# Softmax probabilities of 24 heads kept in one PSUM bank, and a maximum over partitions taken by TensorE

## The chip, the cores and the metric

The kernel runs on one core of a Trainium2 chip. The metric is the time of one execution on the device in microseconds (us); the number quoted is the median of three runs. A separate profiled execution gives the trace from which all rows here are read. The engines are named as in the profile: PE (TensorE, matmuls), DVE (VectorE), ACT (ScalarE), POOL (GpSimd) and SP (SyncE, which here only issues DMAs). "Span" is the time from the first to the last instruction in the trace.

## What is computed

A causal attention with a decay, whose output is the input of a small mixture of experts:

```python
B, H, S, D = 4, 8, 576, 64
scores = q @ k^T / sqrt(D)
scores = where(causal, -1e9, scores + cum[:, :, :, None] - cum[:, :, None, :])   # cum = cumsum(log f)
attn   = exp(scores - max(scores));  attn = attn / (sum(attn) + 1e-9)
x      = (attn @ v)  reshaped to [2304, 512]
p      = domain_probs / (domain_probs.sum(-1) + 1e-9)
out    = sum over e in 0..3 of  p[:, e] * (max(x @ w1[e], 0) @ w2[e])            # w1 512x1024, w2 1024x512
```

The float32 data is multiplied as pairs of a high and a low half (`hi`/`lo`, mostly float16), so that one product is three matmuls. For float16 each tensor is scaled by a power of two, found at run time from the largest magnitude in it.

## The kernel before

**Jobs and heads.** Attention works by job: a batch `b` (0 to 3), a pair of heads `pr` (0 to 3) and a half. A first half is the queries 0 to 255 (tiles 0 and 1 of 128 rows), a second half the queries 256 to 575 (tiles 2, 3, 4). First halves of all four batches run first, then the second halves. A job has two heads, so there are 64 entries in `heads`. Entries 0 to 7 (batch 0) run alone in a start-up; entries 8 to 31 are the first halves of batches 1 to 3, and these 24 heads are what the change speaks of first. They run woven with steps of the expert matmuls: `Step.l1` (L1077, first layer), `Step.gate` (ACT L1090 writes `gh`, DVE L1091 writes `gl`), `Step.l2` (L1113, second layer) and the addition of a finished result to `acc` (DVE, L1137 or L1142).

**One head.** A head of the 24 takes these steps, for tile 0 (128 keys) and tile 1 (256 keys):

- `qk_pe`: two matmuls (L638) put the scores in a PSUM tile `s`. Before the change each query tile has its own `s`, so a head takes two PSUM banks.
- `qk_min`: one custom instruction on DVE (L652) reads `s` and the mask, writes the scaled scores to an SBUF tile `p`, and keeps the row minimum in `nm` (a second small row with the name `nm` reads the accumulator).
- `qk_exp`: ACT (L667) computes the exponential of `p` in place, with `nm` as bias, and sums a row into `ss`.
- `recip16`: DVE turns the two sums of the head into factors `rs` (L702, L705).
- `turn16`: ACT (L748) writes the high half of `p * rs` to the float16 buffer `z`, DVE (L749) the low half; then SP issues two transposing DMAs (L761) that put `z` into `pt`.
- later `av_pair` (PE, L848) multiplies `pt` by v, and `out16` (ACT, DVE L902) splits the result into `y`.

**PSUM.** There are eight banks of 512 float32 columns. `ps_a` has four buffers, which `s`, the attention outputs `o` and a few small tiles (`top...`) take in turn; `ps_1` and `ps_2` have two each, for the two expert layers. The SBUF pool `p_p` for `p` has six buffers.

**Scale of v.** For batches 0 to 3 an upper bound on the attention output is made from v (`x_bound`), batch by batch. Since the second halves use one common scale, `v_scale` (L390) combines them: `top` takes the maximum over the columns of `vmax` (DVE, L398 and L401), which leaves 128 numbers on 128 partitions. To reduce over partitions, SP writes them to DRAM (`dv`, L402) and reads them back as one row copied to every partition (`tops`, L403). `finish` then takes the maximum of that row on DVE, cuts it to a power of two, and makes `vsc` and `xun` (L408 to L421). `weigh` (POOL, L442) for later chunks and the split of v for second halves need the result. `top` belongs to the list `bounds[30]`, `finish` to `bounds[31]`, that is, to the last two of the 24 heads.

The helper `power` (L200) does the same reduction for the bounds of the batches and for the weights: PE transposes the column into a PSUM tile (L206), DVE reduces that row and cuts it to a power of two (L209 to L220), PE multiplies by ones to copy it to all partitions (L227), and DVE reads it (L236, L239).

**Order.** Heads and expert steps are put in a sequence by a planner that paces attention steps between matmuls; from it, a scheduler orders the instructions of each engine when the program is built. Each engine then runs its list strictly in that order, and waits at an instruction until what it needs is there. SP's list is one queue of DMA issues.

Of the kernel before, what the change touches and what calls it, by code (L numbers as in the profile page):

```python
# [85 lines left out]
def fused(ctx: ExitStack, tc: tile.TileContext, qk, v, f, probs, w, out):  # L86
# [42 lines left out]
    xun = const.tile([128, 8], F32, name="xun")  # L129
    tops = const.tile([128, 256], F32, name="tops")  # L130
    pr_r = tops[:, : NT // 128 * E].rearrange("p (t e) -> p t e", e=E)
    ones_r = const.tile([4, 128], F32, name="ones_r")
# [257 lines left out]
    def v_scale():  # L390

        m = vmax[:, NV : NV + 1]
        d = dr_p.tile([128, 1], F32, tag="dv", name="dv", bufs=1)
        u = vmax[:, NV + 1 : NV + 2]

        def top():
            assert all(("x", b) in known for b in range(B))
            nc.vector.tensor_tensor(  # L398
                out=vmax[:, :B], in0=vmax[:, :B], in1=xsc[:, :B], op=ALU.max
            )  # L400
            nc.vector.tensor_reduce(out=m, in_=vmax[:, :NV], op=ALU.max, axis=AX.X)  # L401
            nc.sync.dma_start(out=d, in_=m)  # L402
            nc.sync.dma_start(  # L403
                out=tops[:, :128], in_=d.rearrange("q k -> (q k)").partition_broadcast(128)
            )

        def finish():
            nc.vector.tensor_reduce(out=u, in_=tops[:, :128], op=ALU.max, axis=AX.X)  # L408
            nc.vector.tensor_scalar(out=u, in0=u, scalar1=TINY, scalar2=None, op0=ALU.max)
            nc.vector.tensor_scalar(  # L410
                out=u.bitcast(I32),
                in0=u.bitcast(I32),
                scalar1=EXPONENT,
                scalar2=None,
                op0=ALU.bitwise_and,
            )
            nc.vector.reciprocal(out=vsc[:, B : B + 1], in_=u)
            nc.vector.tensor_scalar(
                out=xun[:, B : B + 1], in0=u, scalar1=2.0**-2, scalar2=None, op0=ALU.mult
            )  # L420
            nc.vector.tensor_scalar(  # L421
                out=vsc[:, B : B + 1],
                in0=vsc[:, B : B + 1],
                scalar1=2.0**14,
                scalar2=None,
                op0=ALU.mult,
            )
            known.add(("x", B))

        return top, finish  # L430

# [81 lines left out]
    class Job:  # L513


        def __init__(self, b, pr, half):
# [4 lines left out]
            self.njt = 2 if half == 0 else 5  # L521
            self.pairs = b > 0 or half > 0
            self.nm = f"{b}_{pr}_{half}"
            self.hi, self.kl, self.q2, self.p, self.nmax = {}, {}, {}, {}, {}
# [86 lines left out]
        def begin(self, hh):  # L611
            for t in self.its:
                self.p[hh, t] = p_p.tile([128, S], F32, tag="p", name=f"p{self.nm}_{hh}_{t}")
            self.nmax[hh] = st_p.tile([128, 8], F32, tag="nmax", name=f"nm{self.nm}_{hh}")
            if hh == 0:
                n = len(self.its)
                self.ssum = st_p.tile([128, 2, n], F32, tag="ssum", name=f"ss{self.nm}")
                self.rs = st_p.tile([128, 2, n], F32, tag="rs", name=f"rs{self.nm}")

        def qk_pe(self, hh, its):  # L620

            at = 512
            for t in its:
# [3 lines left out]
                for n, (a, z) in enumerate(cuts):  # L627
# [4 lines left out]
                    for m, (lhsT, rhs) in enumerate(  # L632
# [11 lines left out]
                        )  # L644
                    self.sp.setdefault((hh, t), []).append((a, z, ps[:, at : at + z - a]))
                    at += z - a

# [28 lines left out]
        def qk_tile(self, hh, t):  # L676
            self.qk_pe(hh, (t,))
            self.qk_min(hh, t)
# [252 lines left out]
    parts_v = v_scale()  # L931
    bounds[30] = [(50, parts_v[0])]
    bounds[31] = [(50, parts_v[1])]

# [901 lines left out]
```

## Time and profile before

| | us |
|---|---|
| median of three runs | 935.0 |
| range of the three | 934.6 to 940.25 |
| the profiled execution | 933.63 |
| its span in the trace | 931.8 |

The 24 heads run from about 53 to about 245 us of the span; in that stretch stands nearly all of PE's idle time after the start-up. In the rows further below, `L652` is a line of the kernel before; `out<-in` names the tiles without their buffer numbers; `x24` is a count; `[10.38 <-DMA tops<-dv]` is idle time of the engine just before the instruction, and what ended it. A wait for several things is put down to the one that came last.

### The profile page before, as it was taken

Reading aid. Unit: us, or ns where it says so; the run is one execution under the profiler, and the core shown is the slowest. Engines: PE = TensorE matmul, PEld = TensorE weight load, DVE = VectorE, ACT = ScalarE, POOL = GpSimd, SP = SyncE. Lnnn points to the kernel's source line nnn. Section 1 sums busy time; section 2 is a strip of 40 time slices with the busy share of each in tenths; the row PEclk is TensorE's granted clock in tenths of the full one; section 3 lists DMA queues with packets and bytes.
Section 4 is the critical chain, followed back from the end, with each engine's and each line's share of the span. In section 5 each row is a group of like instructions: output and inputs, shape, how many; then the busy total and the mean of one; then the engine's idle time right before and its main releaser. Section 6 shows DMA issues by size and latency. Waiting matters only on the chain.

```text
span 931.8 us, 16630 instructions
## 1 busy us (share of the span) xinstructions
PE 866.4 (93%) x5756; PEld 570.8 (61%) x5756; DVE 712.5 (76%) x1496; ACT 544.4 (58%) x1118; POOL 463.9 (50%) x496
## 2 busy tenths in 40 slices
PE   3698989879999998999999899999998999999998
PEld 2577756446667665676766576654455664666547
DVE  5589799836888899878888867655678747786487
ACT  5766849435676685665767765445655345653350
POOL 3746645344325275325238520384778627885060
PEclk9999999989999999999999999999999999999999
DMA  8667889949999999985897984254322422241003
GB/s 281 197 180 235 232 273 250 256 120 270 252 236 258 228 255 276 238 235 125 209 286 228 299 184 76 56 187 140 114 74 91 159 91 89 70 124 36 24 1 91
DMA packets 167236, 163.64 MB, mean 176 GB/s; under 512 B 105108, under 2 KB 129872, under 8 KB 167152
## 3 DMA queue, kind: packets, MB, share of 16 engines
q1 hardware_dynamic: 167152, 162.58, 62.8%
q8 instruction: 45, 0.74, 0.3%
q14 instruction: 39, 0.32, 0.1%
HBM read 116.78 MB, written 21.64 MB: 149 GB/s over the span
## 4 chain that ended last, share of the span: by engine, by line
PE 48%; POOL 9%; DVE 8%; ACT 6%; issue 3%; DMA 1%; SPq 0%; POOLq 0%; ACTq 0%; DVEq 0%
PE l L1077 13%; PE l L1113 13%; PE y L1348 8%; PE m L1348 8%; PE s L638 4%; POOL s L1408 4%; POOL wt L1245 3%; PE o L848 3%; POOL wu L1245 1%; DVE z L749 1%; DVE rl L1234 1%; ACT wt L1272 1%; DVE acc L1142 1%; DVE h L1383 1%; ACT r L1394 1%
## 5 line engine op out<-in xcount | busy, mean ns | idle before, releaser
L1077 PE MATMUL l<-y,w 128*128 128x256 f16 x1728 | 213.9, 274 | 2.1 <-DVE w L1044 2.1
L1077 PEld LDWEIGHTS <-w 128*128 128x128 f16 x1728 | 162.7, 98 | 43.6 <-issue 7.4
L1113 PE MATMUL l<-w,gh 128*128 128x512 f16 x568 | 173.6, 389 | 9.6 <-DVE acc L1142 9.6
L667 ACT ACTIVATE p<-p,nm 128x576 f32<-128x576 f32 (+2 forms) x160 | 95.7, 599 | 87.2 <-DVE nm L652 74.9
L586 POOL CAST q<-raw 64x320 fp32r<-64x320 f32 (+1 forms) x56 | 27.0, 482 | 193.3 <-issue 88.5
L749 DVE SCALAR_TENSOR_TENSOR z<-p,rs,z 128x384 f16<-128x384 f32 (+5 forms) x176 | 109.5, 645 | 16.6 <-ACT z L748 15.3
L1113 PE MATMUL l<-w,gl 128*128 128x512 f16 x284 | 108.4, 387 | 6.9 <-DVE gl L1091 6.9
L748 ACT ACTIVATE z<-p,rs 128x384 f16<-128x384 f32 (+5 forms) x176 | 88.6, 550 | 31.5 <-issue 17.7
L1142 DVE SCALAR_TENSOR_TENSOR acc<-y,scg,acc 128x256 f32<-128x256 f32 (+1 forms) x164 | 81.2, 516 | 14.9 <-PE y L1348 14.7
L1113 PEld LDWEIGHTS <-gh 128*128 128x128 f16 x568 | 51.5, 99 | 60.2 <-issue 19.3
L638 PE MATMUL s<-hi 128*128 128x384 f32 (+1 forms) x192 | 77.1, 409 | 10.9 <-POOL hi L600 5.8
L652 DVE CUSTOM_DVE_ANT_0 p<-s,mask 128x288 f32<-128x288 f32 (+2 forms) x160 | 74.2, 474 | 16.4 <-PE s L638 16.1
L1348 PE MATMUL m<-rh,bs 128*128 128x512 f16 x256 | 86.4, 379 | 0.2 <-POOL bs L1277 0.2
L594 POOL TENSOR_TENSOR kl<-raw,hi 64x576 fp32r<-64x576 f32 (+1 forms) x56 | 66.2, 1182 | 17.8 <-ACT hi L585 17.1
L1277 POOL TENSOR_TENSOR bs<-wt,bs 128x512 f16<-128x512 f32 x32 | 37.9, 1190 | 73.4 <-ACT bs L1276 73.0
L1091 DVE SCALAR_TENSOR_TENSOR gl<-l,gh 128x512 f16<-128x512 f32 (+1 forms) x80 | 54.7, 684 | 16.3 <-ACT gh L1090 15.6
L1348 PE MATMUL m<-rh,bw 128*128 128x512 f16 x191 | 64.5, 379 | 1.0 <-ACT r L1394 0.9
L585 ACT ACTIVATE hi<-raw 128x896 fp32r<-128x896 f32 (+1 forms) x56 | 45.3, 808 | 34.3 <-DMA raw<-in_qk 13.7
L638 PE MATMUL s<-kl,q 66*128 66x384 f32 (+1 forms) x192 | 61.6, 327 | 0.0
L1348 PEld LDWEIGHTS <-bs 128*128 128x128 f16 x384 | 37.5, 98 | 38.8 <-POOL bs L1277 0.7
L1383 DVE SCALAR_TENSOR_TENSOR h<-s,h 128x512 f16<-128x512 f32 x40 | 46.4, 1165 | 17.8 <-ACT h L1382 17.5
L1348 PEld LDWEIGHTS <-h 128*128 128x128 f16 x480 | 46.9, 98 | 14.8 <-issue 2.6
(389 smaller groups left out, 1889.2 us busy)
## 6 DMA issues: line engine op xcount, KB each, us to landing
wr<-in_w SPq DMA_DIRECT2D x74, 512.0 KB
wd<-w SPq DMA_DIRECT2D x32, 512.0 KB
w<-wd SPq DMA_DIRECT2D x32, 512.0 KB
raw<-in_qk SPq DMA_DIRECT2D x32, 448.0 KB
wp<-in_w SPq DMA_DIRECT2D x32, 256.0 KB
bv<-wd SPq DMA_DIRECT2D x32, 256.0 KB
bw<-wd SPq DMA_DIRECT2D x32, 256.0 KB
raw<-in_qk SPq DMA_DIRECT2D x24, 256.0 KB
```

What stands on the lines that cost most here:

```text
L594: eng.tensor_tensor(out=kl[:64, :wk], in0=r[:64, ko : ko + wk], in1=hi[:64, ko : ko + wk].bitcast(F32), op=ALU.subtract,)
L638: nc.tensor.matmul(out=ps[:, at : at + z - a], lhsT=lhsT, rhs=rhs, start=(m == 0), stop=(m == 1),)
L652: nc.vector.tensor_tensor_reduce(out=pt[:, a:z], in0=ps, in1=mask[:, m0 + a : m0 + z], scale=-0.125, scalar=BIG if n == 0 else nm[:, col : ...
L667: nc.scalar.activation(out=pt[:, :w_], in_=pt[:, :w_], func=AF.Exp, scale=-1.0, bias=self.nmax[hh][:, c : c + 1], accum_out=self.ssum[:, h ...
L748: nc.scalar.activation(out=o[:, 0], in_=x, func=AF.Copy, scale=sc)
L749: nc.vector.scalar_tensor_tensor(out=o[:, 1], in0=x, scalar=sc, in1=o[:, 0], op0=ALU.mult, op1=ALU.subtract)
L1077: nc.tensor.matmul(out=self.l1p[:, fi, :], lhsT=lhsT, rhs=rhs[:, k, :], start=(k == 0 and m == 0), stop=(k == 3 and m == 2),)
L1091: self.last = nc.vector.scalar_tensor_tensor(out=self.gl, in0=self.l1p, scalar=0.0, in1=self.gh.bitcast(F32) if wide else self.gh, op0=ALU ...
L1113: matmul(out=l2[tt], lhsT=lhsT, rhs=rhs, start=(opens and fi == 0 and m == 0), stop=(closes and fi == 1 and m == 2),)
L1142: nc.vector.scalar_tensor_tensor(out=acc[c][:, tt, d0:d1], in0=ps, scalar=sc, in1=acc[c][:, tt, d0:d1], op0=ALU.mult, op1=ALU.add,)
L1348: line.append(nc.tensor.matmul(**args))
L1383: nc.vector.scalar_tensor_tensor(out=t[:, 1], in0=x, scalar=0.0 if relu else 1.0, in1=t[:, 0], op0=op, op1=ALU.subtract,)
```

## The change

**First part.** For jobs with `b > 0` and `half == 0` (`stays`), the `p` tiles are not taken. `qk_pe` is called once for both query tiles, so that their scores (128 + 256 = 384 columns) lie side by side in one PSUM bank, and `p` is that piece of PSUM: `qk_min` and `qk_exp` work in place in PSUM, and `turn16` reads PSUM.

**Second part.** `v_scale` uses `power` for the reduction over partitions, so the two DMAs and the buffer `tops` go. It has three parts now, in `bounds[29]` to `bounds[31]`.

```diff
@@ def v_scale():
         m = vmax[:, NV : NV + 1]
-        d = dr_p.tile([128, 1], F32, tag="dv", name="dv", bufs=1)
-        u = vmax[:, NV + 1 : NV + 2]
+        def use(u, r):
+            nc.vector.tensor_scalar(
+                out=xun[:, B : B + 1], in0=u, scalar1=2.0**-2, scalar2=None, op0=ALU.mult
+            )
+            nc.vector.tensor_scalar(
+                out=vsc[:, B : B + 1], in0=r, scalar1=2.0**14, scalar2=None, op0=ALU.mult
+            )
+            known.add(("x", B))
...
             nc.vector.tensor_reduce(out=m, in_=vmax[:, :NV], op=ALU.max, axis=AX.X)
-            nc.sync.dma_start(out=d, in_=m)
-            nc.sync.dma_start(
-                out=tops[:, :128], in_=d.rearrange("q k -> (q k)").partition_broadcast(128)
-            )
-        def finish():
-            nc.vector.tensor_reduce(out=u, in_=tops[:, :128], op=ALU.max, axis=AX.X)
-            nc.vector.tensor_scalar(out=u, in0=u, scalar1=TINY, scalar2=None, op0=ALU.max)
...
-            known.add(("x", B))
-        return top, finish
+        across, exponent, finish = power(1, m, "v", use)
+        return lambda: (top(), across()), exponent, finish
@@ class Job, __init__
+            self.stays = b > 0 and half == 0
@@ def begin
-                self.p[hh, t] = p_p.tile([128, S], F32, tag="p", name=f"p{self.nm}_{hh}_{t}")
+                if not self.stays:
+                    self.p[hh, t] = p_p.tile([128, S], F32, tag="p", name=f"p{self.nm}_{hh}_{t}")
@@ def qk_pe
+                    if self.stays:
+                        self.p[hh, t] = ps[:, at : at + z - a]
@@ def qk_tile
-            self.qk_pe(hh, (t,))
+            if not self.stays:
+                self.qk_pe(hh, (t,))
+            elif t == self.its[0]:
+                self.qk_pe(hh, self.its)
@@
-    bounds[30] = [(50, parts_v[0])]
-    bounds[31] = [(50, parts_v[1])]
+    for n in range(3):
+        bounds[29 + n] = [(50, parts_v[n])]
```

A third edit only renames: `pr_r`, a view of `tops` before, has a tile `pr_t` of its own.

**What moves.** On PE only the instructions from about the 120th to the 2070th stand in another order, which is the stretch of the 24 heads; behind that the lists agree. PE gets two instructions more (a transpose and a matmul for `topv`), SP loses one row (the two DMAs of v; the issue of one other DMA falls into another row), DVE loses one.

DVE, first pair of heads of batch 1 (`s1_0_0_0...` is head 0, `s1_0_0_1...` head 1; the digit after the head is the query tile before the change, while after it both tiles are in one `s`; `ux` is a step of a bound). Before:

```order
L652 ISA p1_0_0_0_0_587,nm1_0_0_0_589<-s1_0_0_0_0_0_657,mask_112 128x128
L652 ISA p1_0_0_0_1_588,nm1_0_0_0_589<-s1_0_0_0_1_0_683,mask_112 128x256
L652 ISA p1_0_0_1_0_702,nm1_0_0_1_704<-s1_0_0_1_0_0_714,mask_112 128x128
L702 TENSOR_SCALAR ss1_0_0_590<-ss1_0_0_590 128x2
L705 RECIPROCAL rs1_0_0_591<-ss1_0_0_590 128x2
L652 ISA p1_0_0_1_1_703,nm1_0_0_1_704<-s1_0_0_1_1_0_731,mask_112 128x256
L749 SCALAR_TENSOR_TENSOR z0_691<-p1_0_0_0_0_587,rs1_0_0_591,z0_691 128x128
L749 SCALAR_TENSOR_TENSOR z0_691<-p1_0_0_0_1_588,rs1_0_0_591,z0_691 128x2x128
```

After:

```order
L637 ISA s1_0_0_0_0_0_656,nm1_0_0_0_588<-s1_0_0_0_0_0_656,mask_112 128x128
L637 ISA s1_0_0_1_0_0_710,nm1_0_0_1_700<-s1_0_0_1_0_0_710,mask_112 128x128
L637 ISA s1_0_0_0_0_0_656,nm1_0_0_0_588<-s1_0_0_0_0_0_656,mask_112 128x256
L637 ISA s1_0_0_1_0_0_710,nm1_0_0_1_700<-s1_0_0_1_0_0_710,mask_112 128x256
L690 TENSOR_SCALAR ss1_0_0_589<-ss1_0_0_589 128x2
L693 RECIPROCAL rs1_0_0_590<-ss1_0_0_589 128x2
L737 SCALAR_TENSOR_TENSOR z0_689<-s1_0_0_0_0_0_656,rs1_0_0_590,z0_689 128x128
L737 SCALAR_TENSOR_TENSOR z1_690<-s1_0_0_1_0_0_710,rs1_0_0_590,z1_690 128x128
L737 SCALAR_TENSOR_TENSOR z0_689<-s1_0_0_0_0_0_656,rs1_0_0_590,z0_689 128x2x128
```

(L637 of after is L652 of before, L690 is L702, L693 is L705, L737 is L749; the rows that only read an accumulator and those of other work are left out.) The minima of the two heads alternate now, tile by tile, and so do the low halves.

ACT at the same place before:

```order
L667 ACTIVATE p1_0_0_0_0_587,ss1_0_0_590<-p1_0_0_0_0_587,nm1_0_0_0_589 128x128
L667 ACTIVATE p1_0_0_0_1_588,ss1_0_0_590<-p1_0_0_0_1_588,nm1_0_0_0_589 128x256
L585 ACTIVATE hi1_1_0_1_759<-raw1_1_0_1_712 128x512
L667 ACTIVATE p1_0_0_1_0_702,ss1_0_0_590<-p1_0_0_1_0_702,nm1_0_0_1_704 128x128
L748 ACTIVATE z0_691<-p1_0_0_0_0_587,rs1_0_0_591 128x128
L748 ACTIVATE z0_691<-p1_0_0_0_1_588,rs1_0_0_591 128x2x128
```

ACT there after:

```order
L652 ACTIVATE s1_0_0_0_0_0_656,ss1_0_0_589<-s1_0_0_0_0_0_656,nm1_0_0_0_588 128x128
L567 ACTIVATE hi1_1_0_1_752<-raw1_1_0_1_708 128x512
L652 ACTIVATE s1_0_0_1_0_0_710,ss1_0_0_589<-s1_0_0_1_0_0_710,nm1_0_0_1_700 128x128
L652 ACTIVATE s1_0_0_0_0_0_656,ss1_0_0_589<-s1_0_0_0_0_0_656,nm1_0_0_0_588 128x256
L652 ACTIVATE s1_0_0_1_0_0_710,ss1_0_0_589<-s1_0_0_1_0_0_710,nm1_0_0_1_700 128x256
L736 ACTIVATE z0_689<-s1_0_0_0_0_0_656,rs1_0_0_590 128x128
```

In the built program DVE and ACT take turns on a bank: the exponential of tile 0 waits for its minimum, the minimum of tile 1 waits for the exponential of tile 0, and so on through the four high and low halves. Over the 24 heads DVE has 23 waits for ACT more than before (164 instead of 141) and ACT 23 for DVE more (104 instead of 81). On PE, the scores of a later head wait for the last low half of an earlier head, since its bank comes free only then; before, they waited for an earlier head's minimum.

DVE at the scale of v before (`acc0` is the evacuation of an expert result, L1142; its `scg` comes from `weigh`):

```order
L749 SCALAR_TENSOR_TENSOR z0_691<-p3_0_0_0_0_2236,rs3_0_0_2240,z0_691 128x128
L408 TENSOR_REDUCE vmax_122<-tops_126 128x1
L409 TENSOR_SCALAR vmax_122<-vmax_122 128x1
L410 TENSOR_SCALAR vmax_122<-vmax_122 128x1
L749 SCALAR_TENSOR_TENSOR z0_691<-p3_0_0_0_1_2237,rs3_0_0_2240,z0_691 128x2x128
L417 RECIPROCAL vsc_123<-vmax_122 128x1
L418 TENSOR_SCALAR xun_125<-vmax_122 128x1
L421 TENSOR_SCALAR vsc_123<-vsc_123 128x1
L1142 SCALAR_TENSOR_TENSOR acc0_1097<-l2_6_6_0_0_0_2381,scg_128,acc0_1097 128x512
L1142 SCALAR_TENSOR_TENSOR acc0_1097<-l2_6_6_0_0_1_2388,scg_128,acc0_1097 128x512
```

DVE at the scale of v after, some 30 instructions later in its list:

```order
L209 TENSOR_REDUCE uv_173<-topv_172 1x1
L555 SCALAR_TENSOR_TENSOR v23_2_0_2569<-vh3_1511,vsc_123,v23_2_0_2569 128x4x64
L637 ISA s3_2_0_1_0_0_2658,nm3_2_0_1_2638<-s3_2_0_1_0_0_2658,mask_112 128x128
L637 ISA nm3_2_0_1_2638 128x1
L210 TENSOR_SCALAR uv_173<-uv_173 1x1
L637 ISA s3_2_0_0_0_0_2597,nm3_2_0_0_2566<-s3_2_0_0_0_0_2597,mask_112 128x256
L637 ISA nm3_2_0_0_2566 128x1
L213 TENSOR_SCALAR uv_173<-uv_173 1x1
L220 TENSOR_SCALAR uv_173<-ident_111,uv_173 1x1
```

The evacuations `acc0` of step 6 no longer stand behind the reduction. `vmax` itself (L401 before) is ready some 65 rows ahead of its transpose on PE, and the result is read (L236) 20 DVE rows behind this reduction.

## Rows read from the trace of the kernel before

**Rows 1.** The page's first part: busy time of each engine over the span.

```profile
PE 866.4 (93%) x5756; PEld 570.8 (61%) x5756; DVE 712.5 (76%) x1496; ACT 544.4 (58%) x1118; POOL 463.9 (50%) x496
```

**Rows 2.** Waits of PE, 53 to 245 us: line, waited for, total us, times, longest.

```profile
PE l L1113 <- DVE acc L1142: 9.4, 3, 6.1
PE l L1113 <- DVE gl L1091: 5.0, 6, 1.5
...
PE topx L227 <- DVE ux L220: 1.8, 2, 1.6
```

**Rows 3.** Windows: length, busy by engine (count), TensorE's granted clock, DMA share, GB/s.

```profile
275.00:300.00 25.00, 25.00 (x184) 17.07 (x181) 21.64 (x55) 16.43 (x34) 16.09 (x17) 1.00 0.90 237
...
168.20:171.70 3.50, 2.95 (x7) 1.04 (x8) 3.50 (x7) 0.79 (x2) 1.13 (x2) 0.51 1.25 239
...
194.30:200.40 6.10, 0.03 (x1) 0.00 (x0) 1.98 (x9) 0.00 (x0) 0.69 (x3) 0.88 0.25 22
200.40:205.80 5.40, 4.62 (x11) 1.41 (x11) 4.70 (x12) 1.47 (x5) 5.40 (x9) 0.50 0.81 188
...
362.40:366.80 4.40, 4.38 (x17) 2.37 (x18) 2.27 (x6) 3.85 (x9) 1.40 (x2) 0.61 0.86 250
```

**Rows 4.** Timeline of PE at three places: start, length, operation, idle before it.

```profile
166.82 0.59 PE L1113 MATMUL l<-w,gh 128*128 128x512 f16 x2 [2.20 <-DVE acc L1142]
...
200.40 1.87 PE L1113 MATMUL l<-w,gh 128*128 128x512 f16 x4 [6.07 <-DVE acc L1142]
...
362.42 0.40 PE L638 MATMUL s<-hi 128*128 128x288 f32 x1 [4.13 <-DVE nm L652]
```

**Rows 5.** Timeline of SP's issues, 186 to 200 us.

```profile
186.88 0.34 SPq L402 DMA_DIRECT2D dv<-vmax  x1
193.81 0.32 SPq L403 DMA_DIRECT2D tops<-dv  x1
194.22 6.40 SPq L761 DMA_TRANSPOSE pt<-z  x2
```

**Rows 6.** Timeline of DVE at two places, about 164 and 187 to 201 us.

```profile
163.90 2.20 DVE L749 SCALAR_TENSOR_TENSOR z<-p,rs,z 128x128 f16<-128x128 f32 x1
...
187.62 0.35 DVE L749 SCALAR_TENSOR_TENSOR z<-p,rs,z 128x128 f16<-128x128 f32 x1
198.35 0.29 DVE L408 TENSOR_REDUCE vmax<-tops 128x1 f32<-128x128 f32 x1 [10.38 <-DMA tops<-dv]
...
199.60 1.41 DVE L1142 SCALAR_TENSOR_TENSOR acc<-l,scg,acc 128x512 f32<-128x512 f32 x2
```

**Rows 7.** Timeline of POOL, at 163.7 us.

```profile
163.70 2.26 POOL L1039 TENSOR_TENSOR w<-wr,w 128x512 f16<-128x512 f32 x2
```

**Rows 8.** DVE's groups, 53 to 245 us: busy us, mean ns, idle before.

```profile
L749 DVE SCALAR_TENSOR_TENSOR z<-p,rs,z 128x128 f16<-128x128 f32 x24 | 12.8, 535 | 1.2 <-ACT z L748 1.2
L749 DVE SCALAR_TENSOR_TENSOR z<-p,rs,z 128x256 f16<-128x256 f32 x24 | 12.7, 531 | 0.1
```

**Rows 9.** DVE's groups, whole span: operations that read PSUM, and two forms of the minimum.

```profile
L1142 DVE SCALAR_TENSOR_TENSOR acc<-y,scg,acc 128x256 f32<-128x256 f32 x140 | 63.5, 477 | 14.9 <-PE y L1348 14.7
L1142 DVE SCALAR_TENSOR_TENSOR acc<-l,scg,acc 128x512 f32<-128x512 f32 x64 | 47.0, 742 | 1.4 <-PE l L1113 0.9
...
L652 DVE CUSTOM_DVE_ANT_0 p<-s,mask,nm 128x288 f32<-128x288 f32 x32 | 16.4, 513 | 2.8
...
L652 DVE CUSTOM_DVE_ANT_0 p<-s,mask 128x288 f32<-128x288 f32 x32 | 14.4, 450 | 8.0 <-PE s L638 7.9
```

**Rows 10.** Waits of DVE, 53 to 245 us: line, waited for, total us, times, longest.

```profile
DVE ss L702 <- ACT p L667: 9.4, 7, 2.5
...
DVE z L749 <- ACT z L748: 1.2, 3, 0.5
```

**Rows 11.** ACT's groups, 53 to 245 us: the exponential of tile 0.

```profile
L667 ACT ACTIVATE p<-p,nm 128x128 f32<-128x128 f32 x24 | 9.4, 392 | 21.0 <-DVE nm L652 16.5 <-DVE uw L239 2.5 <-DVE ux L210 2.0
```

More of the change, by code (lines that the diff above doesn't have):

```diff
@@ L129, in fused @@
     xun = const.tile([128, 8], F32, name="xun")
-    tops = const.tile([128, 256], F32, name="tops")
-    pr_r = tops[:, : NT // 128 * E].rearrange("p (t e) -> p t e", e=E)
+    pr_t = const.tile([128, NT // 128 * E], F32, name="pr_t")
+    pr_r = pr_t.rearrange("p (t e) -> p t e", e=E)
     ones_r = const.tile([4, 128], F32, name="ones_r")
@@ L401, in top @@
             nc.vector.tensor_reduce(out=m, in_=vmax[:, :NV], op=ALU.max, axis=AX.X)
-            nc.sync.dma_start(out=d, in_=m)
-            nc.sync.dma_start(
-                out=tops[:, :128], in_=d.rearrange("q k -> (q k)").partition_broadcast(128)
-            )
-        def finish():
-            nc.vector.tensor_reduce(out=u, in_=tops[:, :128], op=ALU.max, axis=AX.X)
-            nc.vector.tensor_scalar(out=u, in0=u, scalar1=TINY, scalar2=None, op0=ALU.max)
[L410 to L427, printed above, removed]
-            known.add(("x", B))
-        return top, finish
+        across, exponent, finish = power(1, m, "v", use)
+        return lambda: (top(), across()), exponent, finish
     weighed = set()
```

## The prediction

> **What bounds the kernel now.** First the page's busy times: PE works 866.4 us of the span, 93%, and no other engine comes near [rows 1]. So time can be won only where PE stands idle or runs at its lower clock. A table of windows then shows where that is not: at 275 to 300 us PE is busy 25.00 of 25 us [rows 3], and so it is over most of the later stretches. The stretch of the 24 heads is the exception. PE's waits there, 53 to 245 us, are nine groups; seven of them wait for DVE and sum to 19.6 us. Three of them are shown [rows 2]: 9.4 us in 3 waits for the evacuation `acc`, 5.0 us in 6 for `gl`, 1.8 us in 2 for the scale of a batch; the other four sum to 3.4. The timeline of PE shows that one event makes most of the first: 6.07 us ahead of 200.40 us [rows 4]. DVE is the engine waited for, so I then read what DVE waits for and where it is merely slow.
>
> **What stops PE at 200 us.** DVE ends a low half at 187.62 us and then waits 10.38 us for `tops` [rows 6]. The issues on SP say why [rows 5]: `dv` to DRAM goes out at 186.88, the reading back can be issued only at 193.81, and the reduction starts at 198.35. That is 11.5 us for one maximum over partitions. Behind the reduction on DVE stand the two `acc` evacuations of 199.60 us [rows 6]; PE needs their banks and stops. SP's queue is stopped too: the transposes behind the DMA pair go out at 194.22 us. After its pause PE runs at a granted clock of 0.50, the lower of its two levels: in the 5.40 us from 200.40 it is busy 4.62 us [rows 3].
>
> **Term 1: the scale of v.** The change takes out both DMAs and DVE's wait; in the new order the `acc` evacuations stand ahead of the reduction. PE wins its pause, 6.07 us. It also wins what the half clock cost: 4.62 us of work at clock 0.50 would take 2.3 us at full clock, so 2.3 us. Together **−8.4**. What comes in is one transpose and one matmul on PE and three small DVE operations in place of others. The same chain runs seven times before the change (three bounds, four weight scales) and holds PE for 1.8 us in two waits of the batches' bounds [rows 2]; here the transpose stands 65 rows behind the `vmax` that it needs, and the result is read 20 DVE rows after the reduction, so I take 0, with 1 us as the other bound. Who consumes the result, `weigh` for chunk 4 and the v of second halves, stands far behind.
>
> **Term 2: the low half from PSUM.** The 48 low halves of the 24 heads take 535 and 531 ns on the mean [rows 8]. Their own size does not explain that: one that ran alone took 0.35 us, and one took 2.20 us while POOL was in an operation of 2.26 us on two SBUF tiles [rows 6, 7]. So some of them stand still beside POOL. The nearest operation of this form that reads PSUM is the evacuation `acc`, 477 ns for 256 columns and 742 for 512 [rows 9]. It has a second operand in SBUF, as the low half will. From 256 to 512 columns it grows by 265 ns, so from 128 to 256 by half of that, and 128 columns take 477 − 133 = 344 ns, an estimate. DVE then saves 535 − 344 = 191 and 531 − 477 = 54 ns, 24 times each: 24 × 0.245 = 5.9 us. The other bound is 0, if a PSUM source with an SBUF operand beside it stands still as often.
>
> How much of that reaches PE? One place is in rows. The low half of 2.20 us ends where an `acc` evacuation begins, and PE waits 2.20 us for that evacuation and resumes at 166.82 us [rows 4, 6]. With 0.35 in place of 2.20 the wait is 1.85 us shorter. Behind it the clock is 0.51, with 2.95 us of work in the window from 168.20 [rows 3]; if the shorter pause spares that, 2.95 × 0.49 = 1.4 us more. I take both: **−3.3**. Left over on DVE are 5.9 − 1.85 = 4.0 us.
>
> The Trainium skill ("SBUF — State Buffer", section "Who interferes with whom") says that a DVE instruction with two SBUF inputs contends with a GpSimd instruction that reads SBUF, and that one with at most a single SBUF input does not. The 2.20 us beside POOL agree; that the low half from PSUM escapes is shown by no row here, and if it does not, term 2 is 0 and the sum 926.6 on the median.
>
> **Term 3: taking turns on a bank.** Two engines do not work on one bank together in the built program, so DVE gets 23 waits for ACT more. The waits of this kind that exist: 9.4 us for the sums after an exponential (24 instructions) and 1.2 us for the low half after a high half (48 instructions) [rows 10], 10.6 us over 72 instructions, 0.147 us each. For 24 that is 3.5 us. The upper bound is a whole exponential of tile 0, 392 ns [rows 11], 24 times: 9.4 us; the lower is 0, when DVE has other work first, as the alternating order of two heads provides. Queued behind such a waiting minimum are `gl` and `acc`, for which PE waits. At 3.5 us it uses up most of the 4.0 us left over from term 2, so the two together move PE by about **0**.
>
> **Term 4: the minimum written to PSUM.** No row shows this operation with a PSUM output. The nearest: its form with one operand more takes 513 ns for 288 columns, the plain form 450 [rows 9]. I take 0, for the 48 minima, with 48 × 63 ns = 3.0 us as bound to either side. ACT, now from and to PSUM, is not waited for by PE; also 0.
>
> **Term 5: banks.** A head takes one bank of `ps_a`, not two, but keeps it until its last low half. Scores of a later head wait for that. In the new order they stand later in PE's list by up to about 110 rows, so the wait should be over when PE comes there: 0, with the price if not below.
>
> **Sum.** 933.63 − 8.4 − 3.3 = 921.9 on the profiled execution. The median of the runs shown is 935.0, 1.4 above it, so **923** for the median.
>
> **Rivals.**
> *More than that (0.16).* All waits of PE for DVE outside the event at 200 us come to 19.6 − 6.07 = 13.5 us, and the half clock at 168 us costs 1.4. If freed DVE time and the new order, which at `gl5_5_1_0` has 16 DVE instructions fewer ahead, take them all: −8.4 − 13.5 − 1.4 = −23.3, 911.7 on the median. For it: seven of the nine groups of PE's waits are waits for DVE. Against: the instructions return behind that place. Half of it gives 917; this case covers 910 to 917.
>
> *The turns eat it (0.24).* Each of the 24 turns costs 0.392 and the minima 3.0 us more: 9.4 + 3.0 − 5.9 = +6.5 us on DVE, all of it passed to PE: 933.63 − 8.4 + 6.5 + 1.4 = 933.1, within 1% of before. With only the v part coming through, 926.6. For it: DVE and ACT both wait on the path of a head, and 2.5 us were waited for one sum [rows 10]. Against: two heads alternate. The Trainium skill ("PSUM — Partial Sum Buffer", section "PSUM bank collisions raise a hardware error") gives the reason for the turns: accesses of different engines to one bank and partition quadrant must be kept apart, also where addresses differ. The order built here agrees; by this rule alone the change costs time, and no row of before shows how much.
>
> *The change's v part does not come through (inside the case above).* If PE merely waits for what is late next, `gl` at 203 us or a transposed `pt`, a part of the 8.4 remains: half of it makes 927.5.
>
> *Slower (0.08).* A late low half keeps a bank, PE's next scores wait at the head of its list and the expert matmuls behind them with them. The price of one such stop is in rows: at 362.42 us PE waited 4.13 us for a minimum [rows 4], and then worked 4.38 us at clock 0.61 [rows 3], 4.38 × 0.39 = 1.7 us lost; 5.8 us in all. Two stops use up the gain of 11.7; from four on the kernel is over 1% slower (923 + 4 × 5.8 = 946). For it: a bank is held from scores to the last low half, with two heads in flight in four banks that `o` and `top` share. Against: 24 heads with one bank each take 24 buffers where they took 48, and scores stand later in PE's list.
>
> **How the numbers follow.** The forecast, 918 to 928, has 0.52; more 0.16; eaten 0.24; slower 0.08. I take 1% (below 925.7, above 944.4) as about what a measurement of this kernel can tell from no change. Faster: 0.16 and 0.42 of the forecast's 0.52, 0.58. Same: the rest of the forecast, 0.10, and the eaten case, 0.34. Slower: 0.08. The range runs from 910 (all waits gone) to 935 (turns at their bound and a little more); outside it I leave the stops and the far ends, 0.15.
>
> **What will show it.** Right: no wait for `tops`, no PE pause over 2 us near 190 to 205 us and clock 1.00 there; low halves near 344 and 477 ns with no single one over 1 us; waits of DVE for ACT at minimum and low half 3 to 4 us in sum. Wrong: low halves as long as before (term 2 is 0); PE waits for a low half ahead of scores (banks); new PE waits for `gl` or `acc` longer than the 13.5 us of now (turns); minima some 60 ns longer than now (term 4); or second halves that start late because the scale of v came later.

## The result, and the profile after

| | before | after |
|---|---|---|
| median, us | 935.59 | 923.72 |
| range of the runs shown | 934.6 to 940.25 | 921.61 to 924.95 |
| profiled execution | 933.63 | 924.95 |
| its span | 931.8 | 923.2 |

The ratio is 0.9866 with a 95% interval of 0.9841 to 0.9892; measured again in a second set of runs it was 0.9883 (0.9861 to 0.9905). The forecast was 923, with 910 to 935 as the range. The sum came true almost to the microsecond; the runs below show that what lies beyond the scale of v came by other steps than those given.

**Where the time went.** To compare like with like I cut both traces at the same piece of work, the start of the expert matmul with number 1000 (of 4680), which lies behind the last of the 24 heads. The start, 60 us, is a fixed time, at which the kernels have done unequal work (48 expert matmuls before, 41 after). Windows from 60 us to there, before the change (length, busy time by engine, granted clock, DMA share, GB/s):

```profile
60.00:260.20 200.20, 178.54 (x1223) 126.34 (x1222) 163.72 (x408) 123.84 (x292) 97.93 (x122) 0.97 0.83 230
```

and after it, with a second window around the old pause:

```profile
60.00:249.50 189.50, 175.59 (x1235) 127.54 (x1234) 161.82 (x411) 122.22 (x293) 93.07 (x122) 0.99 0.86 243
...
188.00:206.00 18.00, 16.98 (x120) 11.07 (x115) 14.51 (x38) 11.98 (x36) 9.81 (x12) 1.00 0.82 235
```

The stretch is 10.7 us shorter. PE's idle time in it falls from 200.20 − 178.54 = 21.7 to 189.50 − 175.59 = 13.9 us, and its mean clock rises from 0.97 to 0.99. Behind matmul 1000 nothing is won: to the end it takes 931.8 − 260.2 = 671.6 us before and 923.2 − 249.5 = 673.7 after. So the gain lies in the stretch of the 24 heads, though that stretch does not hold nearly all of PE's idle time after the start-up, as I wrote ahead of the prediction, but half of it, 21.7 of 41.4 us (windows of the kernel before):

```profile
245.00:931.80 686.80, 667.11 (x4483) 424.14 (x4481) 523.00 (x1002) 394.37 (x758) 335.95 (x323) 1.00 0.57 155
53.00:245.00 192.00, 170.34 (x1164) 123.06 (x1163) 156.72 (x400) 118.18 (x284) 98.95 (x125) 0.96 0.83 233
```

Around 200 us, where PE stood 6.07 us and then ran at 0.50 [rows 3, 4], it is busy 16.98 of 18 us at clock 1.00. The chain of the v scale is now cheap for PE. Timeline of PE (its transpose and its matmul by ones), after the change:

```profile
207.28 0.27 PE L206 MATMUL topv<-ident,vmax 128*1 128x128 f32 x1
213.44 0.38 PE L227 MATMUL topv<-uv,ones_r 1*128 1x1 f32 x2 [0.26 <-DVE uv L220]
```

PE waits 0.26 us for it, once. For `vsc`, which DVE writes at 218.38 us, POOL waits 2.7 us (`weigh`) and PE does not. The chain itself is hardly shorter: from the transpose to `vsc` it takes 218.53 − 207.28 = 11.3 us, and from the old DMA's issue to the old `vsc` it took 199.67 − 186.88 = 12.8. What is new is that DVE and PE do other work between its steps.

What PE waits for has changed. Its waits from 53 to 245 us after the change (line, waited for, total, times, longest):

```profile
PE o L836 <- DMA pt<-z: 5.4, 5, 1.7
PE l L1101 <- DVE acc L1130: 2.8, 2, 2.3
...
PE s L621 <- DVE z L737: 0.9, 1, 0.9
```

`acc` is down from 9.4 to 2.8 us, `gl` from 5.0 us to no row of the list [rows 2]. In their place stands a wait for transposed probabilities, 9.1 us in the second profiled execution of the same kernel. I had named it only in passing, as what might be late next behind the v scale, and given it no price of its own.

DVE's groups in the same stretch after the change:

```profile
L737 DVE SCALAR_TENSOR_TENSOR z<-s,rs,z 128x256 f16<-128x256 f32 x24 | 11.4, 478 | 7.6 <-ACT z L736 7.3
...
L737 DVE SCALAR_TENSOR_TENSOR z<-s,rs,z 128x128 f16<-128x128 f32 x24 | 8.0, 341 | 3.2 <-ACT z L736 3.1
...
L637 DVE CUSTOM_DVE_ANT_0 s<-s,mask 128x256 f32<-128x256 f32 x24 | 10.1, 425 | 4.3 <-ACT s L652 4.2
...
L637 DVE CUSTOM_DVE_ANT_0 s<-s,mask 128x128 f32<-128x128 f32 x24 | 6.9, 287 | 0.4 <-PE s L621 0.4
```

The low halves take 478 and 341 ns, as worked out (477 and 344); before they took 531 and 535 [rows 8]. But DVE now waits for ACT ahead of them: its last column sums to 10.4 us of waiting for the high half, where it was 1.2 [rows 10]. The chain at 180 us shows why. On ACT, DVE and PE (three timelines), after the change:

```profile
180.40 0.47 ACT L736 ACTIVATE z<-s,rs 128x256 f16<-128x256 f32 x1 [5.42 <-DMA pt<-z]
...
180.91 0.48 DVE L737 SCALAR_TENSOR_TENSOR z<-s,rs,z 128x256 f16<-128x256 f32 x1 [5.20 <-ACT z L736]
...
180.36 0.66 PE L836 MATMUL o<-pt,v 128*64 128x256 f16 x11 [1.58 <-DMA pt<-z]
```

ACT waits 5.42 us to write a high half, because the buffer `z` is still being read by the transposing DMAs of the head pair before; DVE waits behind ACT, 5.20 us. Over the stretch ACT's waits ahead of high halves are, after the change:

```profile
ACT z L736 <- DMA pt<-z: 14.1, 4, 5.4
...
ACT z L736 <- issue: 6.1, 3, 3.0
```

and before it:

```profile
ACT z L748 <- issue: 12.6, 4, 3.9
```

"issue" is a wait for which the profile names nothing. The runs with four buffers `z` below have little or nothing of either kind, so I read both as waits for `z`: it was short before the change too, and is shorter now.

### The profile page after: what moved, and what is told of

Same layout as the page of the kernel before. It is cut to its first block, busy times and chain, and to the rows that moved or that the text cites. A ratio compares the mean times of both kernels' runs of the same rounds, so it can differ in the third digit from the quotient of the medians.

```text
span 923.2 us, 16642 instructions
## 1 busy us (share of the span) xinstructions
PE 863.3 (94%) x5759; PEld 571.8 (62%) x5759; DVE 709.3 (77%) x1498; ACT 542.7 (59%) x1118; POOL 458.8 (50%) x496
## 4 chain that ended last, share of the span: by engine, by line
PE 51%; POOL 10%; DVE 7%; ACT 5%; issue 3%; DMA 2%; SPq 0%; POOLq 0%; ACTq 0%; DVEq 0%
PE l L1101 14%; PE l L1065 14%; PE y L1336 8%; PE m L1336 8%; PE s L621 5%; POOL s L1396 4%; POOL wt L1233 3%; PE o L836 3%; POOL wu L1233 1%; DVE rl L1222 1%; ACT wt L1260 1%; DVE z L737 1%; DVE h L1371 1%; ACT r L1382 1%; DVE acc L1130 1%
## 5 line engine op out<-in xcount | busy, mean ns | idle before, releaser
L652 ACT ACTIVATE p<-p,nm 128x384 f32<-128x384 f32 (+3 forms) x112 | 74.4, 665 | 60.3 <-DVE nm L637 52.8
L737 DVE SCALAR_TENSOR_TENSOR z<-p,rs,z 128x384 f16<-128x384 f32 (+3 forms) x128 | 83.8, 679 | 15.7 <-ACT z L736 14.5
L736 ACT ACTIVATE z<-p,rs 128x384 f16<-128x384 f32 (+3 forms) x128 | 69.5, 590 | 8.8 <-issue 4.0
L637 DVE CUSTOM_DVE_ANT_0 p<-s,mask 128x384 f32<-128x384 f32 (+3 forms) x112 | 58.4, 529 | 15.3 <-PE s L621 15.1
L1078 ACT ACTIVATE gh<-l 128x512 f16<-128x512 f32 (+1 forms) x80 | 46.9, 586 | 16.5 <-PE l L1065 16.3
```

The source lines that it names most:

```text
L637: nc.vector.tensor_tensor_reduce(out=pt[:, a:z], in0=ps, in1=mask[:, m0 + a : m0 + z], scale=-0.125, scalar=BIG if n == 0 else nm[:, col : ...
L652: nc.scalar.activation(out=pt[:, :w_], in_=pt[:, :w_], func=AF.Exp, scale=-1.0, bias=self.nmax[hh][:, c : c + 1], accum_out=self.ssum[:, h ...
L736: nc.scalar.activation(out=o[:, 0], in_=x, func=AF.Copy, scale=sc)
L737: nc.vector.scalar_tensor_tensor(out=o[:, 1], in0=x, scalar=sc, in1=o[:, 0], op0=ALU.mult, op1=ALU.subtract)
```

## The experiments

Ratios are to the kernel before, run on the same chip. "Idle" is PE's idle time from 60 us to expert matmul 1000, length less busy time, "at 1000" is when that matmul starts, and "clock" is the mean granted clock between, all in the one profiled execution.

| kernel | ratio | 95% interval | idle, us | at 1000, us | clock |
|---|---|---|---|---|---|
| before | 1 | | 21.7 | 260.2 | 0.97 |
| changed | 0.9866 | 0.9841 to 0.9892 | 13.9 | 249.5 | 0.99 |
| changed, again | 0.9883 | 0.9861 to 0.9905 | 12.2 | 251.8 | 0.97 |
| v_only: v part alone | 0.994 | 0.9917 to 0.9963 | 12.6 | 252.4 | 0.96 |
| psum_only: PSUM part alone | 0.9987 | 0.9966 to 1.0009 | 17.0 | 254.4 | 0.96 |
| two_banks: both parts, a bank per tile | 0.999 | 0.9973 to 1.0006 | 15.3 | 257.7 | 0.96 |
| sbuf_p: v part, one bank, p in SBUF | 0.9878 | 0.985 to 0.9907 | 10.6 | 249.6 | 0.96 |
| both_first: the same, a bank per tile | 0.9955 | 0.9932 to 0.9977 | 15.7 | 256.4 | 0.97 |
| one_bank_late: one bank, scores in turn | 0.993 | 0.9911 to 0.995 | 14.4 | 252.6 | 0.96 |
| four_z: changed, four buffers z | 0.9892 | 0.987 to 0.9914 | 8.4 | 250.3 | 0.96 |
| paced: changed, costs corrected | 0.9878 | 0.9853 to 0.9902 | 12.8 | 250.8 | 0.97 |
| sbuf_paced: sbuf_p, costs corrected | 0.989 | 0.9867 to 0.9913 | 14.5 | 250.3 | 0.99 |
| v_four_z: v part, four buffers z | 0.9909 | 0.9891 to 0.9928 | 15.3 | 254.4 | 0.97 |
| sbuf_four_z: sbuf_p, four buffers z | 0.9811 | 0.9786 to 0.9836 | 6.4 | 240.5 | 0.99 |

The idle column alone does not sort the kernels: `v_only` has less idle time than the changed kernel and a lower clock, and is slower. The start of matmul 1000, which holds both, does so in the main. It comes from one execution each, and that of `v_only` was the fastest of its eight, that of the changed kernel the slowest of its four.

Each edit is followed by a new order of some hundred instructions, since the scheduler orders the program anew; the two `paced` runs below show how much that alone moved. For the changed kernel again:

> The changed kernel as it is, on the chip of the runs beside it, to compare with them: a ratio to before of 0.987 as measured at first. If its gain were an accident of that chip or of single executions, above 0.992.

It was 0.9883, so the gain is no accident of the first runs.

### The two parts apart

`v_only` is the kernel before with the new `v_scale` and its three places in `bounds`, and nothing else.

> The kernel before with the second part alone (the scale of v by TensorE); the probabilities stay in SBUF. If term 1 is right and the parts add up: PE's pause of 6.07 us and the half clock behind it go, 8.4 us less, about 927 us, a ratio of 0.991, and the low halves keep their 535 and 531 ns. Rival, the two parts need each other (the 'acc' evacuations come late for another reason, such as DVE's load): a new pause of PE of 3 us or more between 185 and 205 us, and at most 4 us won, 931 us or more.

Measured: 0.994. Windows of `v_only`, to the same matmul and around the old pause:

```profile
60.00:252.40 192.40, 179.78 (x1235) 128.80 (x1234) 166.30 (x406) 122.26 (x289) 96.32 (x122) 0.96 0.84 239
...
188.00:206.00 18.00, 17.72 (x134) 11.64 (x132) 11.89 (x29) 10.75 (x30) 9.47 (x12) 1.00 0.71 217
```

PE is busy 17.72 of 18 us there, at full clock: the pause and the half clock at that place are gone, and no new pause came between 185 and 205 us. The stretch is 7.8 us shorter and the idle time 9.1 us. The low halves stay long (527 and 703 ns). The price of the place is confirmed; over all its runs the kernel won less than that, 0.6% of 933 us or 5.6 us, 3.5 to 7.7 by the interval, the profiled execution being the fastest of them.

What stayed is the other place of the prediction, that of term 2. PE, DVE and a window of `v_only`:

```profile
165.69 0.59 PE L1094 MATMUL l<-w,gh 128*128 128x512 f16 x2 [3.46 <-DVE acc L1123]
...
159.36 3.12 DVE L1025 SCALAR_TENSOR_TENSOR w<-wr,wsc,w 128x512 f16<-128x512 f32 x1
...
169.00:174.00 5.00, 5.00 (x18) 2.50 (x17) 3.27 (x9) 0.80 (x2) 0.00 (x0) 0.50 0.91 243
```

PE waits 3.46 us for `acc`, longer than the 2.20 us of before, and works at 0.50 afterwards. DVE is late there not by a low half but by a weight operation of 3.12 us and, behind it, a small one of 2.03 us; beside each of them POOL spends 2.26 us on two operations with two SBUF tiles. The changed kernel has no stop of PE over 1.6 us between 135 and 245 us.

`psum_only` is the changed kernel with the DRAM version of `v_scale`.

> The changed kernel with the scale of v through DRAM as before. If terms 2 and 3 are right: about 3 us less than before, 932 us, a ratio of 0.997 with the low halves at 341 and 478 ns and the wait for 'tops' still there. Rival, the turns on a bank cost PE more than the low halves give: 936 us or more. Second rival, the new order alone gives more: 928 us or less.

Measured: 0.9987, about 1 us, with an interval that holds no gain at all and also the 3 us. The low halves are as expected, 342 and 477 ns. Where PE waits instead stands in its trace. PE's waits, `psum_only`:

```profile
PE o L855 <- DMA pt<-z: 13.6, 8, 4.1
```

and PE's longest stop, with DVE's wait for `tops` beside it (two timelines):

```profile
191.66 0.27 PE L855 MATMUL o<-pt,v 128*64 128x256 f16 x1 [4.13 <-DMA pt<-z]
...
194.30 0.28 DVE L408 TENSOR_REDUCE vmax<-tops 128x1 f32<-128x128 f32 x1 [6.55 <-DMA tops<-dv]
```

Here the DRAM round trip no longer stops `acc` but coincides with late transposes, and PE waits for `pt` 13.6 us in all, where the kernel before waited 1.0. The product of the two ratios, 0.994 × 0.9987 = 0.993, is worse than both parts together (0.987 and 0.988) by some 4 to 6 us, a little more than the intervals leave open. The parts seem to help each other.

### Where the probabilities lie

`sbuf_p` keeps the v part, the one bank and both scores at once, but p in SBUF:

```diff
-                if not self.stays:
-                    self.p[hh, t] = p_p.tile(...)
+                self.p[hh, t] = p_p.tile(...)
...
-                    if self.stays:
-                        self.p[hh, t] = ps[:, at : at + z - a]
```

> The changed kernel, scores of both tiles in one bank, but the probabilities in SBUF tiles as before: minimum from PSUM to SBUF, exponential and both halves in SBUF. It takes away the PSUM source of the low half and the turns, and keeps the v part. If POOL beside two SBUF operands is what made the low half long: 128 and 256 columns back above 480 ns on the mean, with single ones over 1 us, and the time 2 to 4 us above the changed kernel, 926 to 928 us. Rival, the length came from the place in the order: low halves stay near 340 and 470 ns. If the turns cost PE more than the low halves give, it is faster than the changed kernel: 921 us or less.

Measured: 0.9878, the same as the changed kernel. DVE's low halves in `sbuf_p`:

```profile
L735 DVE SCALAR_TENSOR_TENSOR z<-p,rs,z 128x256 f16<-128x256 f32 x24 | 13.9, 579 | 0.4 <-ACT z L734 0.3
...
L735 DVE SCALAR_TENSOR_TENSOR z<-p,rs,z 128x128 f16<-128x128 f32 x24 | 11.8, 491 | 1.6 <-ACT z L734 1.6
```

They are long again, as POOL beside two SBUF operands would make them. The single rows bear that out. In `sbuf_p` the low halves that overlap no POOL instruction take 338 ns (11 of 24 with 128 columns, the longest 352) and 477 (13 of 24 with 256 columns); those that overlap one take 620 and 700, up to 1227. In the changed kernel both kinds take the same, 341 and 341, 480 and 476. So reading PSUM does not make a low half faster; it keeps POOL from holding it up.

On balance that gains the kernel nothing that can be measured, but not because PE does not notice. PE's waits in `sbuf_p`:

```profile
PE l L1099 <- DVE gl L1077: 9.2, 3, 4.4
PE o L834 <- DMA pt<-z: 0.9, 1, 0.9
...
PE l L1099 <- DVE acc L1123: 0.5, 1, 0.5
```

For `gl` and `acc` PE waits 9.7 us here and 2.8 in the changed kernel (1.0 in its second profile); for `pt` it waits 0.9 here and 5.4 there (9.1). The pair `paced` and `sbuf_paced` below differs to the same sides: 5.3 and 5.6 us with p in SBUF, 0 and 10.0 in PSUM. In these profiles late transposes take back what DVE wins by its shorter low halves. So the 5 to 7 us that the changed kernel has over `v_only` are not a net gain of the shorter low halves. They come with what `sbuf_p` shares with it: one bank for a head, filled in one go.

### Banks, or both scores at once

`two_banks` is the changed kernel with `qk_pe` called tile by tile again, so that each tile takes a bank which it holds to its low half.

> The changed kernel with a bank of its own for each query tile: the minimum of tile 1 and the exponential of tile 0 need not take turns, but a head holds two banks until its low halves are done. If the turns cost little on PE, and banks are what counts: PE's scores wait for low halves, several stops of 1 to 4 us, 930 to 945 us. Rival, the turns cost PE time: waits of DVE for ACT fall from some 16 us towards 10 us between 53 and 245 us, and the time goes to 921 us or less.

Measured: 0.999. The whole gain is lost, that of the v part too. PE's waits in it:

```profile
PE s L621 <- DVE y L887: 5.3, 3, 3.7
PE o L833 <- DVE z L734: 3.0, 1, 3.0
```

PE stands before an output until a low half has left a bank, 3.0 us, which is the stop of my slower rival, and before scores until DVE has emptied a bank of an output (`y` is the split of `o`), 3.7 us at the longest. DVE's waits for ACT did not fall: 9.6 us for the sum and 6.4 for the high half, 16.0 against 15.9 in the changed kernel. So the rival of the expectation, that the turns between the tiles cost the time, finds nothing here.

`both_first` is `sbuf_p` with a new bank for each tile:

```diff
             for t in its:
+                at = 512 if self.stays else at
```

> Probabilities in SBUF and the v part by TensorE, as in the kernel where both tiles' scores lay in one bank (0.988), but here each tile has a bank of its own again; both tiles' scores are still issued at the first tile. If the one bank per head is what gave 5.7 us over the v part alone: 0.994. If the order (both scores at once) gave it: 0.988.

`one_bank_late` is `sbuf_p` with the scores of tile 1 put into the bank of tile 0, but issued at their own turn:

```diff
+            if self.stays and its[0] == 1:
+                at, ps = 128, self.bank[hh]
...
-            if not self.stays:
-                self.qk_pe(hh, (t,))
-            elif t == self.its[0]:
-                self.qk_pe(hh, self.its)
+            self.qk_pe(hh, (t,))
```

> Probabilities in SBUF and the v part by TensorE, both tiles of a head in one bank, but the scores of the second tile are issued at their own turn, as before the change. If the one bank per head gave the 5.7 us: 0.988. If issuing both scores at once gave them: 0.994. A third way, with one bank the scores of tile 1 must wait until DVE's minimum of tile 0 has left the bank: new waits of PE for 'nm' ahead of scores, and 0.995 or more.

Measured: 0.9955 and 0.993, both about what the v part gives alone. Neither half of the edit wins by itself. PE's waits in `both_first`:

```profile
PE s L622 <- DVE nm L636: 4.4, 1, 4.4
...
PE s L622 <- DVE ux L236: 3.3, 1, 3.3
```

Two banks asked for at once are not free, and PE stands 7.7 us before scores. ACT's waits in `one_bank_late`:

```profile
ACT p L653 <- DVE nm L638: 30.3, 21, 3.8
```

It waits 30.3 us for minima in 21 places, against 16.5 in 10 in `sbuf_p`. But `both_first` has 30.9 us of this wait and the fastest kernel below, `sbuf_four_z`, 33.1, so it explains nothing. The sign of the third way of the expectation, PE waiting for `nm` ahead of scores, is there with 1.5 us only. PE's largest wait in this run is 7.1 us for `pt`. Why scores in turn lose the gain stays open.

Is all this the luck of an order? `paced` and `sbuf_paced` change the planner's costs only:

```diff
-                qs.append((TOK0[t] + 328, ...
+                d = (784, 0)[t] if j.stays else TOK0[t] + 328
+                qs.append((d, ...
```

> The changed kernel with the planner's costs of the two score steps corrected to what they now issue: 784 for the first (both tiles), 0 for the second, instead of 328 and 456. Nothing but the order of some 300 PE instructions changes. It shows what the order alone is worth: if the difference of 5 us and more between the runs with one bank, two banks, both scores at once or not is a matter of banks, this stays within 0.003 of the changed kernel's 0.987. If orders as such move the time by several us, it is off by more than 0.004 in either direction.

> The same correction of the planner's costs for the kernel with one bank, both scores at once, and the probabilities in SBUF (0.988). If banks and not the luck of an order made that kernel 5.7 us faster than the v part alone, it stays between 0.985 and 0.991. If it was luck, it goes towards the 0.994 of the v part alone.

Measured: 0.9878 and 0.989. Some 300 to 400 differing lines in the order of PE's matmuls move the time by 0.001, in both kernels. Two draws are few, but they speak against the luck of an order, and for the edit: one bank, filled at once. They do not say by which path it wins. In `v_only`, where a head takes two banks, PE hardly waits for one: 0.8 us in all ahead of scores.

### The buffer z

`four_z` gives the 24 heads four buffers, two of them idle until the second halves:

```diff
+            zi = hh + 2 * (self.pr % 2) if self.stays else hh
...
-                zs[hh][:, :256],
-                zs[hh][:, 256:768],
+                zs[zi][:, :256],
+                zs[zi][:, 256:768],
```

> The changed kernel with four float16 buffers 'z' in the 24 heads instead of two: odd pairs use the two that stand idle until the second halves. In the trace of the changed kernel ACT waits 14.1 us for the transposing DMAs that still read 'z', DVE waits 10.4 us for ACT's high half behind that, and PE waits 5.4 us for a transposed 'pt'. If the buffer 'z' is the cause: ACT's wait for the DMA is gone, DVE's wait for the high half falls to 3 us or less, PE's wait for 'pt' to 2 us or less, and the time falls by 3 to 5 us against the changed kernel, a ratio of 0.983 to before. Rival, the waits come from the turns on a bank: DVE's wait for the high half stays near 10 us and the time as well. Second rival, the transposes are late in SP's queue anyway: the wait for 'pt' stays.

Two of the three waits went as expected (that for `pt` did not reach 2 us), the time did not: 0.9892. DVE's waits in `four_z`:

```profile
DVE s L637 <- ACT s L652: 2.7, 3, 1.8
DVE z L738 <- ACT z L737: 2.6, 5, 0.8
...
DVE ss L690 <- ACT s L652: 2.1, 3, 1.2
```

ACT's wait for the DMA is no longer listed, DVE's wait for the high half is 2.6 instead of 10.4 us, and PE's wait for `pt` 3.6 instead of 5.4 or 9.1. PE's idle time in the stretch fell from 13.9 (12.2 in the other execution) to 8.4 us. What it gave back: the mean clock in the stretch was 0.96, where the changed kernel had 0.99 and 0.97, and PE's waits before 60 us were nearly 3 us longer than in the kernel before (`s` for `hi` 5.2, `l` for `xh` 3.7 us in that profile). Whether that is bound to this order or was an accident of one execution stays open.

`sbuf_four_z` is the same edit on `sbuf_p`.

> One bank per head with both scores at once, the v part by TensorE, probabilities in SBUF, and four buffers 'z' as in the run four_z. Against four_z (0.989) only the place of the probabilities differs, and neither waits for a transpose that still reads 'z'. If keeping them in PSUM is worth what term 2 says (3 us): 0.992. If it is worth nothing on PE: 0.986 to 0.990, with low halves near 490 and 580 ns all the same.

Measured: 0.9811, 916.07 us: faster than both ways of the expectation, than both kernels, and than every other one here. Its window, and DVE's low halves:

```profile
60.00:240.50 180.50, 174.08 (x1238) 127.99 (x1237) 155.32 (x409) 122.67 (x290) 95.75 (x122) 0.99 0.90 255
```

```profile
L736 DVE SCALAR_TENSOR_TENSOR z<-p,rs,z 128x256 f16<-128x256 f32 x24 | 14.9, 621 | 0.2
...
L736 DVE SCALAR_TENSOR_TENSOR z<-p,rs,z 128x128 f16<-128x128 f32 x24 | 10.6, 443 | 4.9 <-ACT z L735 4.5 <-DMA wr<-in_w 0.4
```

The stretch ends 9.0 us earlier than in the changed kernel, idle 180.50 − 174.08 = 6.4 us, though the low halves are the long ones. With four buffers, probabilities in SBUF are better than in PSUM by 0.8% (0.9811 against 0.9892, intervals apart). By which wait the buffers win here is not shown: in `sbuf_p` ACT waited 2.6 us for DMAs that still read `z` and 9.2 us for nothing named, of which 2.1 us are left, but PE's largest gain is at `gl`, 2.7 instead of 9.2 us. To see if the buffers alone do it, `v_four_z` puts them on `v_only`.

> The v part alone (0.994), probabilities in SBUF and a bank for each query tile as before the change, with the four buffers 'z'. If four buffers are worth 7 us wherever the probabilities lie in SBUF (0.988 to 0.981 with one bank): 0.987. If they pay only together with one bank per head, or if the 0.981 was mostly a good order: 0.992 to 0.996.

Measured: 0.9909, between the two answers: 0.3% better than `v_only`, with intervals that overlap. With one bank the four buffers gain 0.7% (0.9878 to 0.9811, intervals apart). So they gain together with one bank; whether they do without it is within the noise. How much of the 0.9811 is a good order I can't say; the same edit gave nothing on the PSUM kernel.

## Why the prediction was right, and where its steps were not

**Term 1, the scale of v: right.** The pause of 6.07 us and the half clock behind it went, in `v_only` as in the changed kernel, and nothing came in their place at 190 to 205 us. `v_only` shows 7.8 us less to matmul 1000 for the forecast 8.4. That `vsc` comes 19 us later than before was a sign of being wrong, if second halves start late for it; behind matmul 1000 `v_only` takes 672.4 us and `psum_only`, with the old scale, 673.0, so it costs nothing here. Over all runs the v part is worth 5.6 us (3.5 to 7.7): a profile of one execution prices a place, but another execution can differ elsewhere. The changed kernel itself had a mean clock of 0.99 in the stretch in one execution and 0.97 in the other (`after_again`, its window to the same matmul):

```profile
60.00:251.80 191.80, 179.64 (x1244) 131.34 (x1244) 160.89 (x411) 122.58 (x293) 93.27 (x122) 0.97 0.85 241
```

**Term 2, the low half from PSUM: size right, worth wrong.** 341 and 478 ns against 344 and 477, and no low half of the 24 heads over 1 us, where four were. The failed step is the one that brought it to PE: "One place is in rows ... I take both: −3.3." The place is calm in the changed kernel, but the sum has no term for what takes the gain back, the wait for `pt`; `sbuf_p` has the long low halves and the same time. The rule of the Trainium skill ("SBUF — State Buffer", section "Who interferes with whom"), that a DVE instruction with two SBUF inputs contends with a GpSimd instruction that reads SBUF, agrees with these rows, long beside POOL with two SBUF operands (620 and 700 ns) and short with one (341 and 476).

**Term 3, the turns: its sign did not come, and the net was larger, by another cause.** I had named as a sign 3 to 4 us of DVE's waits for ACT at minimum and low half; they are 4.2 and 10.4, 14.6 us. With 1.3 for the sum they make 15.9, where 10.6 were before: 5.3 more in place of 3.5. But with four buffers `z` they are 2.6 + 2.7 + 2.1 = 7.4, below the 10.6 of before. So the turns that the page "PSUM — Partial Sum Buffer" (the Trainium skill, section "PSUM bank collisions raise a hardware error") leads to hardly cost here, and the buffer `z` does, which I had not listed among the resources. Its readers are DMAs on SP. That DVE's alternating between two heads hides the turns, and makes both heads of a pair end late and together, is my reading; no run takes the alternation away.

**Term 4, the minimum: 0 was nearly right.** The minima are 425 and 287 ns, 13 and 8 more than before. What I had not thought of is the row behind them, below.

**Term 5, banks: priced at 0, and it holds a gain.** I priced the longer hold of a bank at 0 and saw no gain. The part beyond the v scale hangs on one bank for both tiles, filled at once: 0.994 without it, 0.988 with it, in SBUF as in PSUM, and 0.999 in PSUM where two banks are held. That is shown by the runs that undo it; by which wait of PE it comes is not shown, and without the v part, in `psum_only`, it gave nothing clear of noise. I had seen that 24 heads take 24 buffers where they took 48, but used it only as an argument against the slower rival.

**The rivals.** The turns did not eat the gain; `two_banks` shows the slower rival's stop, 3.0 us for a low half and 3.7 for an output where I had priced a wait of 4.13, and the one bank keeps it off. That errors in terms 2, 3 and 5 cancelled is luck, and the range of 910 to 935 is what held.

## What to carry to other kernels

Look for the gain of a change in every resource that it takes less of (here a PSUM bank), not only in the operation that it speeds up; then undo one part at a time, since a kernel can be faster for the part that nobody thought of. If two engines are to write a buffer that DMAs read, count how many head pairs can be in flight in it: two buffers more took 8 us off DVE's waits for ACT here and nothing off the time of the changed kernel, but together with one bank per head and probabilities in SBUF they made the fastest kernel (916 us). A pause of PE read from one trace is a price with a few us of doubt: two profiles of the changed kernel differ by 2.3 us at the same matmul, at mean clocks of 0.99 and 0.97.

## What the runs showed of the hardware that was not expected

A small row follows each minimum and reads its accumulator. With the minimum written to SBUF it took 79 ns (before, 53 to 245 us); with most of them written to PSUM, it takes more. DVE, 70 to 240 us after the change (48 rows, 6 of them behind minima that still go to SBUF):

```profile
L637 DVE DVE_READ_ACCUMULATOR2_ANT nm<- 128x1 f32 x48 | 6.2, 129 | 0.0
```

(48 × 129 − 6 × 79) / 42 = 136 ns, 57 more. Over 48 minima that is 2.7 us, nearly term 4's bound of 3.0, from another place. ACT won: its exponentials in place, 392 ns for 128 columns in SBUF [rows 11], take in PSUM

```profile
L652 ACT ACTIVATE s<-s,nm 128x256 f32<-128x256 f32 x24 | 10.7, 447 | 11.7 <-DVE nm L637 6.8 <-DVE ss L690 2.9 <-DVE wtop L361 1.0
...
L652 ACT ACTIVATE s<-s,nm 128x128 f32<-128x128 f32 x24 | 7.9, 330 | 4.3 <-DVE ux L210 2.1 <-DVE nm L637 2.0 <-DVE ux L220 0.2
```

330 ns. What that is worth to PE, which waits for ACT's high halves only by way of DVE and `pt`, no run here tells apart.
